# Routed attention with eight experts: three edits to the order of VectorE's weight sums and of one count

## The chip, the core and the metric

The kernel runs on one core of a Trainium2 chip. A core has five engines that work at the same time, each with an instruction queue of its own that is worked off strictly in order: TensorE (PE: matrix products, with the loading of its weights, PEld, shown apart), VectorE (DVE: elementwise work, reductions, transposes of 32x32 blocks), ScalarE (ACT: activations and copies), GpSimd (POOL: here constants, gathers and scatters by index) and SyncE (SP: starts the transfers between HBM and the on-chip memory). An engine that needs a result of another one waits for it at the head of its queue, and all that is queued behind waits too. The metric is the time of one execution on the device, in microseconds (us).

## The reference, cut to what matters

```python
# attention: batch 4, 8 heads, 768 positions, head size 64, 16 clusters per head
mask = q_assign[:, :, :, None] == k_assign[:, :, None, :]   # same nearest centroid
attn = softmax(where(mask, q @ k.T / sqrt(64), -1e9))
x = (attn @ v)                      # -> 3072 rows of 512
# experts: 8 experts, 512 -> 1024 -> 512, each row goes to one expert
logits = x @ w_gate;  e = argmax(logits);  gate = softmax(logits)[e]
out = gate * (relu(x @ w1[e]) @ w2[e])
```

All inputs and outputs are float32. How many rows each expert gets is known only while the kernel runs.

## The kernel before, in words

**Attention.** 16 head pairs are worked through one after the other; TensorE makes scores (L433), ScalarE the exponentials (L445), VectorE their sums (L451), TensorE the weighted values (L457). While the pairs run, a row's expert is chosen for each batch of 768 rows (`gate`, `choose`), and `count` (L588) and `number` (L595) give each row its place in a list per expert: `count` is two small products on TensorE over the tile `last` that `choose` leaves (L592, L593), `number` is a few small VectorE instructions on the two products and six scatters on GpSimd. For the last batch these steps lie in the expert part, in turn 0.

**Experts in turns.** Ten turns follow, `s` from 0 to 9. A turn takes one expert and a fixed number of its rows: 288 and 288 for the two early turns (chosen by the counts of the first three batches), then 256, 288, 288, 384, 416, 416, 448 and 128 for the experts in order of their counts. Turn s has

- `first_weights` and `second_weights`: SyncE fetches w1 and w2 (2 MB each) into one of two buffers, by s odd or even (L97, L105);
- `places`, `indices`, `gather`, `weigh`, `take`: the list of rows is loaded (L712, L716), VectorE turns it into indices `gi` and `si` (L728, L729), GpSimd gathers the rows (L738), VectorE scales them (`xw`, L755), SyncE stores them to HBM (`turn_rows` in HBM, L761) and loads them again in a blocked layout (`xs`, L771);
- `turn_rows`: one VectorE transpose of `xs` to `xT` (L780);
- `layer1`, then `layer2`.

**Fewer products by sums.** Both layers multiply 2x2 blocks in the seven-product form that needs sums of blocks first. All sums are VectorE instructions at L789: four of the rows (`x_sums`: `xc`), four of the first weights (`w1_sums`: a0 to a3, 128x1024 each), four of the hidden values (`h_sums`: `hs`) and four of the second weights (`w2_sums`: v0 to v3, 128x1024 each). In this order a2 comes before a1 before a3, and v0 before v1 before v3. The first layer uses d = A2 X2 first, then A1, A0 and A3; the second V2, V1, V0 and V3. Each of these tiles has one buffer, so a sum of turn s+1 also waits until turn s has used its own. Turn 0 uses the plain form in its second layer, turn 9 in both.

**Where the products meet VectorE.** In `layer1` each half j makes seven products (L969). The fifth, `product(c, A[0], X[0])`, is followed by a VectorE addition into the hidden tile `h` (L927 by way of `add`), and the seventh goes on adding into the same PSUM bank c, so it waits for that addition. `layer2` has the same shape (L1070): after the fifth product, `product(c, t[0], V[0])`, VectorE adds into `z` (L1138), and the seventh, `product(c, t[3], b22)`, waits for this addition. Those two places are where a late VectorE holds TensorE.

**What sets the order.** Apart from register loads, the order on each queue is the order in which the program calls. `layer1` and `layer2` take lists of hooks. `layer1` calls hook 0 to 6 after the seven products of the first half and 7 to 13 after those of the second, `layer2` calls 0 to 6 after the seven products of its first pair of 128-row blocks (hooks behind that follow whole 128-row blocks); in turn 0, whose second layer is plain, hooks 0 to 3 lie in the first 128-row block and 4 to 7 in the second, one after every second step. `at(h1, i, f, ...)` hangs step f of any turn on hook i of this turn's first layer, `at(h2, i, ...)` on one of its second. Steps on one hook are called in the order of their `at`. For the weight sums the hooks come from a tuple, in the order that the loop at L1220 has: a2, a1, a0, a3, v2, v0.

```python
                if GR[s + 1]["T"] >= 2 * P:
                    for (h, i), f, a in zip(when, (w1_sums,) * 4 + (w2_sums,) * 2, (2, 1, 0, 3, 2, 0)):
                        at(h, i, f, s + 1, (a,), nc.vector)
                at(h2, 1 if s == 1 else 3, turn_rows, s + 1)
                if GR[s + 1]["T"] >= 2 * P:
                    at(h2, 1 if s == 1 else 4, x_sums, s + 1)
```

So before the change VectorE works off, within `layer2` of a turn s >= 2 and for the next turn: a0 (hook 1), a3 and v2 (hook 2), the transpose `xT` (3), the addition into `z` behind the fifth product, `x_sums` and `weigh` (4), the second addition into `z`, v0 (5). In turn 0: a2 (hook 1), a1 (2), `xT` (3), `x_sums` (4), a0 (5), a3 (6), then `indices` of turn 2, v2 and v0 (7).

Of the kernel before, what the change touches and what calls it, by code (L numbers as in the profile page):

```python
# [33 lines left out]
def kernel(  # L34
# [12 lines left out]
    B, H, S, D = q.shape  # L47
# [120 lines left out]
    with tc.manual_schedule(), ExitStack() as actx:  # L168
# [596 lines left out]
        def take(s):  # L765

            g = GR[s]
            T, C = g["T"], g["C"]
            g["xs"] = xp.tile([P, T_MAX // Q4, P], F32, name="xs")
            for r in range(HP):  # L770
                nc.sync.dma_start(  # L771
                    out=g["xs"][Q4 * r : Q4 * (r + 1), 0:C, :],
                    in_=g_d[s][0:T, P * r : P * (r + 1)].rearrange("(c t) d -> t c d", t=Q4),
                )
# [120 lines left out]
    with tc.manual_schedule(), ExitStack() as ectx:  # L895
# [125 lines left out]
        def pairs_of(s):  # L1021


            return GR[s]["T"] // (2 * P) if s else 0

        def h_sums(s):

            g = GR[s]
            g["H"] = []
            for p in range(pairs_of(s)):  # L1030
                c0 = 2 * P * p
                h = g["h"]
                a11, a21 = h[:, 0:4, c0 : c0 + P], h[:, 0:4, c0 + P : c0 + 2 * P]
                a12, a22 = h[:, 4:8, c0 : c0 + P], h[:, 4:8, c0 + P : c0 + 2 * P]
                t = [hpool.tile([P, 4, P], F32, name=f"hs{i}") for i in range(4)]
                V = nc.vector
                strassen(V, t[2], a11, a21, ALU.subtract)
                strassen(V, t[0], a21, a22, ALU.add)
                strassen(V, t[1], t[0], a11, ALU.subtract)
                strassen(V, t[3], a12, t[1], ALU.subtract)  # L1040
                g["H"].append((a11, a12, a22, t))
# [119 lines left out]
        def first_weights(s):  # L1161
            if s >= len(EARLY):
                expert(s)
            GR[s]["w1"] = fetch1(GR[s]["e"], (wa, wb)[s % 2])

        def second_weights(s):
            GR[s]["w2"] = fetch2(GR[s]["e"], (wa, wb)[s % 2])

        for s in range(NS):
            h1, h2 = {}, {}  # L1170

            def at(d, i, f, *a):
                d.setdefault(i, []).append(lambda: f(*a))

            if s == 0:
                at(h1, 3, sum_up, n - 1)
                at(h1, 3, weights_of, n - 1)
                at(h1, 4, gate, B - 1)
                at(h1, 4, gate_exp, B - 1)
                at(h1, 5, gate_sum, B - 1)  # L1180
                at(h1, 5, choose, B - 1)
                at(h1, 8, count, B - 1)
                at(h1, 9, number, B - 1)
                at(h1, 11, rows, n - 1)
                at(h1, 11, store, n - 1)
                at(h1, 12, rank_all)
                at(h2, 0, rank_rest)
                at(h2, 3, places, 2)
                at(h2, 3, first_weights, 2)
                at(h2, 5, places, 3)  # L1190
                at(h2, 7, indices, 2)
                at(h2, 7, gather, 2)
            if s == 3:
                at(h1, 12, ask)
                at(h2, 4, answer)
            if s < last:
                if s == 0:
                    first_weights(1)
                elif s > 1:
                    take(s + 1)  # L1200
                if s == 1:
                    at(h1, 6, weigh, 2)
                    at(h1, 7, take, 2)
                    at(h1, 8, second_weights, 2)
                else:
                    second_weights(s + 1)
                if 0 < s <= last - 2:
                    at(h2, 0, first_weights, s + 2)

                if 0 < s <= last - 3:  # L1210
                    at(h2, 1, places, s + 3)

                if s == 0:
                    when = ((h2, 1), (h2, 2), (h2, 5), (h2, 6), (h2, 7), (h2, 7))
                elif s == 1:
                    when = ((h1, 9), (h1, 12), (h2, 2), (h2, 3), (h2, 6), (h2, 6))
                else:
                    when = ((h1, 9), (h1, 10), (h2, 1), (h2, 2), (h2, 2), (h2, 5))
                if GR[s + 1]["T"] >= 2 * P:
                    for (h, i), f, a in zip(when, (w1_sums,) * 4 + (w2_sums,) * 2, (2, 1, 0, 3, 2, 0)):  # L1220
                        at(h, i, f, s + 1, (a,), nc.vector)
# [3 lines that stand above are left out]
            if s == 0:  # L1225
                at(h1, 2, gather, 1)
                at(h1, 8, weigh, 1, slice(0, 1))
                at(h1, 11, weigh, 1, slice(1, 2))
                at(h1, 12, weigh, 1, slice(2, 3))
                at(h1, 12, take, 1)  # L1230
            elif s + 2 <= last:
                at(h1, 5 if s == 2 else 4, indices, s + 2)
                at(h1, 5 if s == 2 else 4, gather, s + 2)
                at(h2, 6 if s == 1 else 4, weigh, s + 2)
            if pairs_of(s):
                at(h1, 4, w2_sums, s, (1,), nc.vector)

                at(h1, 5 if s == 1 else 6, w2_sums, s, (3,), nc.vector)
            if s == last - 1:

                at(h1, 4, nc.gpsimd.drain)
            (layer1 if GR[s]["T"] >= 2 * P else few_columns)(s, h1)
            h_sums(s)
            layer2(s, h2)
# [271 lines left out]
```

## Time and profile before

| | |
|---|---|
| three executions | 657.41 to 657.73 us, median 657.68 us |
| the profiled execution | 657.44 us, of which the span from first to last instruction is 655.7 us |
| granted TensorE clock | 0.999 of full speed |
| attention, to the first expert product | 0 to 328.2 us of the span |
| expert part | 328.2 to 655.7 us |
| busy in the expert part (328.0 to 655.7) | PE 318.5, PEld 263.5, DVE 203.3, ACT 95.8, POOL 86.9 us |
| span behind TensorE's last product | from about 649.1 us |

How to read it: an engine's busy time is the sum of its instructions' durations, which overlap a little at their ends. TensorE's products are pipelined, their ends are modelled and reach into the next product, so what TensorE loses is read best from the distance between the starts of two groups of products: eight products with the same shape have the same distance from the start of one group to that of the next when nothing is waited for. A line of the timeline has the start, the duration (of all that is merged into the line), engine, source line, operation, the tile written and the tiles read, the shapes, the count, and in square brackets the idle time ahead of it with what ended it. a0 to a3 show as `a`, v0 to v3 as `v`, since buffer numbers are left out.

### The profile page before, as it was taken

What the parts mean: (1) busy time and instruction counts of PE and PEld (TensorE: products, weight loads), DVE (VectorE), ACT (ScalarE), POOL (GpSimd) and SP (SyncE); (2) the same over time, 40 slices, a digit from 0 to 9 for tenths busy, and PEclk for the clock granted to TensorE, in tenths of its full rate; (3) what the DMA queues carried; (4) which work ended last, traced back from release to release, by engine and by line L of the source; (5) the groups of instructions that cost most, each with busy time, mean ns of one, the idle gap of its engine ahead of it and who ended that gap; (6) DMA issues with size and microseconds to landing.
All of it is one profiled execution on the core that took longest, in us unless ns stands there. A gap on an engine that the chain in (4) does not pass through costs nothing.

```text
span 655.7 us, 11490 instructions
## 1 busy us (share of the span) xinstructions
PE 643.5 (98%) x4252; PEld 423.0 (65%) x4252; DVE 489.5 (75%) x845; ACT 338.3 (52%) x584; POOL 133.0 (20%) x166
## 2 busy tenths in 40 slices
PE   8999999999999999999999999999999999999995
PEld 4454544445444454444494989989897977869773
DVE  6988878998889988999977987888869365572300
ACT  5677877768778677867532433334241331413210
POOL 5500000022000300033013612324241422140010
PEclk9999999999999999999999999999999999999999
DMA  7753445443455433329476498667694836614010
GB/s 150 162 104 73 79 92 98 74 80 62 79 98 98 74 74 72 74 33 334 110 274 195 152 335 283 232 254 234 241 309 157 281 131 184 229 66 168 8 49 19
DMA packets 189760, 95.38 MB, mean 145 GB/s; under 512 B 152895, under 2 KB 171839, under 8 KB 188416
## 3 DMA queue, kind: packets, MB, share of 16 engines
q1 hardware_dynamic: 184624, 81.56, 45.4%
q0 software_dynamic: 4928, 12.97, 6.0%
q8 instruction: 35, 0.57, 0.4%
q14 instruction: 29, 0.24, 0.1%
q10 hardware_dynamic: 144, 0.03, 0.0%
HBM read 74.10 MB, written 20.70 MB: 145 GB/s over the span
## 4 chain that ended last, share of the span: by engine, by line
PE 94%; DVE 4%; issue 0%; ACT 0%; POOL 0%; POOLq 0%; DVEq 0%; ACTq 0%
PE sps L433 24%; PE mps L457 19%; PE bank L969 12%; PE bank L1089 10%; PE sbank L969 9%; PE bank L1070 7%; PE sbank L1070 6%; PE mps L480 3%; PE mps L291 2%; PE bank L938 1%; DVE xT L780 1%; DVE a L789 1%; DVE v L789 1%; PE sps L356 0%; PE sps L226 0%
## 5 line engine op out<-in xcount | busy, mean ns | idle before, releaser
L445 ACT ACTIVATE A<-sps 128x768 f32<-128x768 f32 x192 | 151.7, 814 | 29.1 <-PE sps L433 28.5
L433 PE MATMUL sps<-qT,kT 64*128 64x384 f32 x768 | 158.9, 492 | 0.0
L451 DVE TENSOR_TENSOR acc<-acc,A 128x768 f32<-128x768 f32 x128 | 121.3, 948 | 10.6 <-ACT A L445 2.4
L457 PE MATMUL mps<-A,v_in 128*64 128x384 f32 x768 | 127.4, 488 | 0.0
L433 PEld LDWEIGHTS sps<-qT,kT 64*128 64x128 f32 x768 | 66.8, 187 | 52.2 <-issue 46.0
L457 PEld LDWEIGHTS mps<-A,v_in 128*64 128x64 f32 x768 | 53.8, 137 | 70.6 <-issue 64.2
L1044 POOL DMA_INDIRECT out_dram<-z,si x30 | 47.1, 1571 | 195.3 <-DVE z L927 165.7
L607 POOL DMA_INDIRECT tokens_of<-tg,pos_i x24 | 28.2, 1176 | 268.5 <-DVE pos_i L605 262.4
L433 PE MATMUL sps<-mq,mk 64*128 64x384 bf16 x384 | 64.6, 323 | 1.6 <-DVE mk L383 1.0
L1089 PE MATMUL bank<-w,h 128*128 128x512 f32 (+2 forms) x224 | 64.4, 596 | 0.0
L340 ACT ACTIVATE mk<-ohT,kscn,ksc 32x384 bf16<-32x384 bf16 x60 | 42.0, 700 | 40.2 <-DVE ohT L327 36.3
L738 POOL DMA_INDIRECT xg<-x_rows,gi x30 | 40.3, 1343 | 45.8 <-DVE si L729 16.5
L969 PE MATMUL sbank<-xc,a 128*128 128x144 f32 (+4 forms) x288 | 47.9, 309 | 0.2 <-ACT sbank L1002 0.2
L969 PE MATMUL bank<-xT,w 128*128 128x144 f32 (+4 forms) x288 | 47.6, 308 | 0.0
L1089 PEld LDWEIGHTS bank<-w,h 128*128 128x128 f32 (+2 forms) x224 | 24.6, 151 | 32.5 <-issue 32.3
L969 PEld LDWEIGHTS bank<-xT,w 128*128 128x128 f32 x288 | 43.8, 190 | 2.3 <-issue 1.9
L451 DVE TENSOR_TENSOR acc<-A 128x768 f32<-128x768 f32 x32 | 30.6, 957 | 18.3 <-ACT A L445 18.2
L969 PEld LDWEIGHTS sbank<-xc,a 128*128 128x128 f32 x288 | 43.3, 190 | 0.7 <-ACT sbank L1002 0.4
L927 DVE TENSOR_TENSOR h<-sbank,p 128x288 f32<-128x288 f32 (+4 forms) x18 | 9.2, 513 | 45.3 <-PE sbank L969 43.9
L987 ACT ACTIVATE h<-h 128x288 f32<-128x288 f32 (+4 forms) x36 | 17.6, 488 | 40.2 <-DVE h L927 38.1
L433 PEld LDWEIGHTS <-mk 64*128 64x128 bf16 x384 | 19.9, 94 | 27.5 <-DVE mk L383 2.6
L755 DVE TENSOR_TENSOR xw<-xg,sf 128x256 f32<-128x256 f32 (+2 forms) x60 | 32.6, 603 | 0.2
(216 smaller groups left out, 898.7 us busy)
## 6 DMA issues: line engine op xcount, KB each, us to landing
w<-in_moe_w_dram SPq DMA_DIRECT2D x20, 2048.0 KB
v_in<-in_v_dram SPq DMA_DIRECT2D x32, 192.0 KB
x_rows<-x SPq DMA_DIRECT2D x64, 96.0 KB
turn_rows<-xw SPq DMA_DIRECT2D x23, 256.0 KB
q_in<-in_q_dram SPq DMA_DIRECT2D x60, 96.0 KB
k_in<-in_k_dram SPq DMA_DIRECT2D x60, 96.0 KB
xs<-turn_rows SPq DMA_DIRECT2D x16, 144.0 KB
xs<-turn_rows SPq DMA_DIRECT2D x8, 208.0 KB
```

The source lines that it names most:

```text
L340: nc.scalar.activation(dst, src, AF.Identity, bias=less, scale=big)
L433: nc.tensor.matmul(SP[n, h, j][:, a, 0:HS], lhsT=kt[rows, j * P : (j + 1) * P], rhs=qt[rows, h * HS : (h + 1) * HS], start=first, stop=not ...
L445: nc.scalar.activation(A[n, h, j], ps[:, :, 0:HS], AF.Exp, scale=D**-0.5)
L451: nc.vector.tensor_tensor(ACC[n, h], first, A[n, h, j], op=ALU.add)
L457: nc.tensor.matmul(O[n, h][D * a : D * (a + 1), 0:HS], lhsT=VIN[n][:, a, j, :], rhs=A[n, h, j][:, a, :], start=(j == 0), stop=(j == NQ - 1),)
L607: ins = nc.gpsimd.indirect_dma_start(out=t_d[:, :], out_offset=bass.IndirectOffsetOnAxis(ap=pos_i[:, i : i + 1], axis=0), in_=tg[:, b, i, ...
L738: nc.gpsimd.indirect_dma_start(out=xg[0:m], out_offset=None, in_=x_d[0:rows_in, :], in_offset=bass.IndirectOffsetOnAxis(ap=g["gi"][0:m, j ...
L755: nc.vector.tensor_tensor(xw[0:m, :, :, d2 * a : d2 * (a + 1)], xg[0:m].rearrange("p (r a d b) -> p a r b d", r=HP, a=2, b=DB)[:, a], g["s ...
L969: nc.tensor.matmul(ps[:, f * T2 : (f + 1) * T2], lhsT=w[:, k, (2 * j + f) * P : (2 * j + f + 1) * P], rhs=x[:, k, :], start=first and f + ...
L1044: ins = nc.gpsimd.indirect_dma_start(out=out[:, :], out_offset=bass.IndirectOffsetOnAxis(ap=GR[s]["si"][0:rows, j : j + 1], axis=0), in_=z ...
L1070: nc.tensor.matmul(ps[:, 0:H], lhsT=x[:, k, :], rhs=y[:, k, :], start=first and k == 0, stop=k == 3, skip_group_check=not first,)
L1089: nc.tensor.matmul(ps[i * m : (i + 1) * m, :], lhsT=h[:, f, j * P : j * P + m], rhs=w[:, f, :], start=(k == 0), stop=(k == FB // n - 1),)
```

## The change

Three edits, all in the loop over the turns; no instruction is added or taken away, and no shape is changed.

1. Turn 0, first layer: `count` of the last batch goes from hook 8 to hook 9 and `number` from 9 to 10. On TensorE the two small products now follow the third product of the second half instead of preceding it; the order on the other engines does not change by this.
2. Turn 0, second layer, sums for turn 1: a1 goes from hook 2 to 1, a0 from 5 to 2, a3 from 6 to 2, v2 from 7 to 6. VectorE now has a2, a1, a0, a3, then `xT`, the additions into `z`, `x_sums`, v2, the indices of turn 2, v0.
3. Turns s >= 2, second layer, sums for turn s+1: v2 goes from hook 2 to 5, v0 from 5 to 6. VectorE now has a0, a3, `xT`, the addition into `z`, `x_sums`, `weigh`, the second addition into `z`, v2, v0.

The sums in turn 1 (for turn 2) stay where they are. SyncE's order differs at one place: in turn 3 the three stores of weighed rows now stand ahead of a register load for the branch at the end (L1249). GpSimd's and ScalarE's order does not change.

```diff
-                at(h1, 8, count, B - 1)
-                at(h1, 9, number, B - 1)
+                at(h1, 9, count, B - 1)
+                at(h1, 10, number, B - 1)
...
                 if s == 0:
-                    when = ((h2, 1), (h2, 2), (h2, 5), (h2, 6), (h2, 7), (h2, 7))
+                    when = ((h2, 1), (h2, 1), (h2, 2), (h2, 2), (h2, 6), (h2, 7))
                 elif s == 1:
                     when = ((h1, 9), (h1, 12), (h2, 2), (h2, 3), (h2, 6), (h2, 6))
                 else:
-                    when = ((h1, 9), (h1, 10), (h2, 1), (h2, 2), (h2, 2), (h2, 5))
+                    when = ((h1, 9), (h1, 10), (h2, 1), (h2, 2), (h2, 5), (h2, 6))
```

## The prediction

> **What bounds the kernel now.** First the page: busy time by engine and the chain that ended last.
>
> ```profile
> PE 643.5 (98%) x4252; PEld 423.0 (65%) x4252; DVE 489.5 (75%) x845; ACT 338.3 (52%) x584; POOL 133.0 (20%) x166
> ...
> PE 94%; DVE 4%; issue 0%; ACT 0%; POOL 0%; POOLq 0%; DVEq 0%; ACTq 0%
> ```
>
> TensorE is busy for 98% and is 94% of the chain; the 4% of VectorE in it are places where TensorE waited for VectorE. So an edit that only moves VectorE work is worth what it adds to or takes from TensorE's waits. The waits of TensorE between 328 and 656 us are few:
>
> ```profile
> PE sbank L1070 <- DVE z L927: 1.2, 4, 0.4
> PE mps L592 <- DVE last L586: 0.6, 1, 0.6
> PE sbank L969 <- DVE h L927: 0.5, 1, 0.5
> ```
>
> A fourth row is 0.2 us behind ScalarE. These three are the places that the three edits touch. Then I read the timeline at each. Turn 0, TensorE alone:
>
> ```profile
> 336.61 1.14 PE L969 MATMUL bank<-xT,w 128*128 128x144 f32 x8
> 337.59 1.14 PE L969 MATMUL bank<-xc,a 128*128 128x144 f32 x8
> 339.33 0.17 PE L592 MATMUL mps<-last,lt_b 128*128 128x8 bf16 x1 [0.59 <-DVE last L586]
> 339.35 0.17 PE L593 MATMUL mps<-last,ones_b 128*128 128x8 bf16 x1
> 339.38 1.23 PE L969 MATMUL sbank<-xc,a 128*128 128x144 f32 x8
> ```
>
> Groups of this shape start 0.98 us apart (336.61, 337.59); the one around the count starts 1.79 later. Now VectorE from turn 0 into turn 1:
>
> ```profile
> 355.81 1.38 DVE L780 STREAM_TRANSPOSE xT<-xs 128x1152 f32<-128x1152 f32 x1 [3.67 <-DMA xs<-turn_rows]
> ...
> 361.52 1.22 DVE L789 TENSOR_TENSOR a<-w 128x1024 f32<-128x1024 f32 x1
> 362.65 1.22 DVE L789 TENSOR_TENSOR a<-w,a 128x1024 f32<-128x1024 f32 x1
> ...
> 363.93 2.35 DVE L789 TENSOR_TENSOR v<-w 128x1024 f32<-128x1024 f32 x2
> 366.20 0.45 DVE L927 TENSOR_TENSOR h<-sbank,p 128x288 f32<-128x288 f32 x1
> ```
>
> And TensorE over the same stretch:
>
> ```profile
> 365.05 1.14 PE L969 MATMUL bank<-xc,w 128*128 128x144 f32 x8
> 366.71 1.25 PE L969 MATMUL sbank<-xT,a 128*128 128x144 f32 x8 [0.52 <-DVE h L927]
> ```
>
> VectorE idles 3.67 us for the rows, later does four sums in a row, and the addition into h behind them holds TensorE: 1.66 from start to start instead of 0.98. Last, a later turn (4), VectorE and then TensorE:
>
> ```profile
> 466.27 1.21 DVE L789 TENSOR_TENSOR v<-w 128x1024 f32<-128x1024 f32 x1
> 467.40 1.76 DVE L780 STREAM_TRANSPOSE xT<-xs 128x1536 f32<-128x1536 f32 x1
> 469.10 0.37 DVE L927 TENSOR_TENSOR z<-sbank,p 128x256 f32<-128x256 f32 x1
> ```
>
> ```profile
> 467.19 1.89 PE L1070 MATMUL bank<-v,h 128*128 128x256 f32 x8
> 469.52 1.99 PE L1070 MATMUL sbank<-w,hs 128*128 128x256 f32 x8 [0.44 <-DVE z L927]
> ```
>
> 2.33 from start to start, where 1.73 is usual for this shape. The idle column says 0.44, since the modelled end reaches 0.16 into the next group; starts are the better measure, and I use them.
>
> **Edit 1, the count.** 1.79 - 0.98 = 0.81 us lost, of which about 0.1 are the two products themselves, which stay. `last` is ready at 339.27; one group later TensorE arrives at 338.57 + 0.98 = 339.55. So 0.70 goes. What comes behind: `number` starts on VectorE with `base` at 340.22, behind a row weighing that ends at 340.32; the counts will be done near 339.85, so that weighing hides them with 0.4 to spare. Without it VectorE would wait, and with it the transpose and store of the attention rows, by at most the 0.98 of the group. Gain 0.70.
>
> **Edit 2, turn 1's sums.** a0 and a3 leave the place behind `x_sums` (two starts 1.13 apart, 2.27 in all) and fall into the 3.67 idle: a2 starts at 349.68, a1 1.24 later at 350.92, and with two more starts 1.13 apart and 1.22 for the last the four end at 354.4, 1.4 before the rows arrive. Were the rows there already, `xT` would come up to 2.27 later than it could. a0 and a3 wait only for turn 0's first layer, over at 344.4. v2 passes ahead of the indices of turn 2, but these still come 2.27 - 1.13 = 1.14 earlier. The addition into h is wanted at the end of the fifth group, 364.07 + 1.14 = 365.2; VectorE gets there at 366.20 - 2.27 = 363.9. So the whole 1.66 - 0.98 = 0.68 goes, and 1.3 of margin stays for TensorE being 0.70 earlier. A rule of the Trainium skill speaks against this: VectorE: DVE Perf Modes, section "The DRAIN you can't avoid", gives each VectorE instruction a flush of its duration less 266 ns before the next one. Taken as added to the row's 1.21, four sums would take 4 x (1.21 + 0.94) = 8.6 us and end at 358.3, 2.5 behind the rows, and turn 1's second product, which needs `x_sums`, would be late by about as much, 2 us at most. The rows decide: 361.52 and 362.65 start 1.13 apart, so nothing is added.
>
> **Edit 3, v2 behind the rows' turning.** Excess of the seventh group of layer 2, start to start less 1.73: turn 2 0.30 (410.38, 412.40), turn 3 0.08, turn 4 0.61, turn 5 none, turn 6 0.38 (538.89, 541.00), turn 7 0.51 (580.08, 582.32). Together 1.88. v2 takes 1.13 ahead of `xT`, in turn 2 also 1.95 of waiting for w2. Without it `xT` ends at about 468.0 in turn 4, the addition into z at 468.3, and TensorE wants it at 468.92; turns 2, 3, 6 and 7 come out with 0.7 to 1.1 to spare. The rows must be there: in turns 2 to 4 their load is issued 13.9 to 20 us before `xT`, and in turn 0 it took 4.5. What is next late: v2 and v0 now stand back to back ahead of the next turn's addition into h, but `weigh` too is about 1.13 earlier. In turn 3, with the distances of today's rows: a3 ends at 437.9, `xT` at 439.2, the addition into z waits for its product until 439.37, the small steps of `answer` and `x_sums` put `weigh` at 442.0, the second addition at 445.2, v2 at 445.5, v0 at 446.65, and it ends at 447.87; the addition into h is wanted at 447.96 - 0.08 = 447.88. The same sum gives v0's end at 418.5 in turn 2 (wanted 419.1) and 476.8 in turn 4 (wanted 477.5); turns 5 to 7 have a whole 128-row block (6.9 us) in between. Turn 3 is a tie, and its addition has about 0.2 to give before TensorE feels it (done at 448.42, next group at 448.67). Cost 0; with no cover at all it is 1.13 for each of the three turns.
>
> **Queues.** The moved sums issue no DMA. On SyncE three stores pass a register load that waits until 441.2; the stores go at 444.11: nothing. On GpSimd the scatter behind the addition into z now meets v2 and v0. The Trainium skill's page SBUF — State Buffer, section "Who interferes with whom", infers that tensor_tensor leaves GpSimd's writing of descriptors alone; here scatters beside sums back to back take 3.92 us (435.91) where 0.97 is usual. By the rule the next gathers come when they do now, by the row up to 3 us later; rows gathered are weighed some 10 to 20 us later, so both give 0. Only turn 2's gather is close: 5.7 us from indices to weighing, of which both ends move up by 1.1 to 1.4.
>
> **Sum.** 0.70 + 0.68 + 1.88 = 3.26. Profiled execution 657.44 - 3.26 = 654.18; it lies 0.24 under the median of the runs, so the median should be 657.68 - 3.26 = 654.4. Turn 1's own wait (385.34 to 387.39, 0.32) and one for ScalarE in turn 3 (0.37) stay; if they go too, 653.7.
>
> **Rivals.** *A, all seven waits go*: 654.4. *B, the lead of 1.38 from turns 0 and 1 is given back in turn 2*: its v2 waits for w2 until 388.18, so VectorE is tied to a transfer there. If w2 doesn't come earlier, `weigh` and the addition into h follow it and TensorE waits. For it: DMA share 0.90 from 374.5 to 389. Against: w2's issue (377.69) stands behind the row stores and loads of `weigh`, which moves up 1.3. Time 654.4 + 1.4 = 655.8. *C, the change does less than it says*: the waits are worth only the idle column, 0.59 + 0.52 + 0.44 + 0.22 + 0.35 = 2.12, and B happens to the first two (1.11): 657.68 - 1.01 = 656.7. Against: distances between starts are longer. *D, slower*: transfers, not VectorE, set when `xT` starts. Then it stays where it is, the old waits stay, and v0 ends 1.13 later, less VectorE's present idle before h, 0.74, 0.32 and 0.76: 0.39 + 0.81 + 0.37 = 1.57, so 659.2. It decides from the point where the rows land within 0.3 us of today's `xT`; the 13.9 us and more speak against it, what speaks for it is DMA share 0.96 in turn 2.
>
> **Numbers.** A 0.62, B 0.17, C 0.11, D 0.10. Below 657.68 by over 0.2% (1.3 us, about what can be told from no change) are A and B, 0.79; C within, 0.11; D 0.10. The range goes from 653.6 (A with the two waits that stay) to 656.8 (through B and C).
>
> **What would show it.** Right: the three VectorE rows of TensorE's waits gone or down to turn 1's; the count with no idle before it; 0.98 into the seventh group of turn 1; `xT` of turn 4 right behind a3; VectorE with idle ahead of the next h. Wrong: `xT` waiting for the rows in turns 2 to 7, TensorE waiting for h in turns 2 to 5, or v of turn 2 waiting longer for w2.

## The result, and the profile after

The median goes from 657.69 us (six executions, 657.08 to 658.26) to 653.73 us (six, 652.92 to 654.72): ratio 0.994, 95% interval 0.9928 to 0.9952, or 3.96 us less. The profiled execution took 653.81 us, with a span of 652.0.

The page's rows on busy time and on the chain that ended last, after:

```profile
PE 642.6 (99%) x4252; PEld 423.6 (65%) x4252; DVE 490.1 (75%) x845; ACT 339.1 (52%) x584; POOL 138.9 (21%) x166
...
PE 97%; DVE 1%; issue 0%; POOL 0%; POOLq 0%; ACT 0%; DVEq 0%
```

No engine does less work. VectorE's share of the chain fell from 4% to 1% and TensorE's rose from 94% to 97%: what went is waiting. TensorE's waits between 326 and 656 us, after:

```profile
PE sbank L1070 <- DVE z L927: 0.2, 1, 0.2
```

One row is left of the three (and the one behind ScalarE): turn 1's own wait, which the edits do not touch. The count in turn 0, TensorE:

```profile
339.33 1.14 PE L969 MATMUL sbank<-xc,a 128*128 128x144 f32 x8
340.31 0.17 PE L592 MATMUL mps<-last,lt_b 128*128 128x8 bf16 x1
340.34 0.17 PE L593 MATMUL mps<-last,ones_b 128*128 128x8 bf16 x1
340.37 1.23 PE L969 MATMUL bank<-xT,w 128*128 128x144 f32 x8
```

The two small products have no idle ahead of them. From 339.33 to 340.37 are 1.04 us where 1.79 were. VectorE from turn 0 into turn 1:

```profile
353.23 1.22 DVE L789 TENSOR_TENSOR a<-w,a 128x1024 f32<-128x1024 f32 x1
355.85 1.38 DVE L780 STREAM_TRANSPOSE xT<-xs 128x1152 f32<-128x1152 f32 x1 [1.39 <-DMA xs<-turn_rows]
...
365.32 0.46 DVE L927 TENSOR_TENSOR h<-sbank,p 128x288 f32<-128x288 f32 x1 [1.27 <-PE sbank L969]
```

The sums a0 (at 352.10) and a3 (the first line) now lie in what was VectorE's idle time ahead of the rows. The addition into h has 1.27 us of idle ahead of it, put down to TensorE: now VectorE waits for TensorE. Over the same stretch TensorE starts its groups 0.98 apart, the one that waited among them:

```profile
365.05 1.14 PE L969 MATMUL bank<-xc,w 128*128 128x144 f32 x8
366.03 1.14 PE L969 MATMUL sbank<-xT,a 128*128 128x144 f32 x8
```

Last, turn 4, VectorE and then TensorE:

```profile
463.12 1.21 DVE L789 TENSOR_TENSOR a<-w,a 128x1024 f32<-128x1024 f32 x1
464.26 1.76 DVE L780 STREAM_TRANSPOSE xT<-xs 128x1536 f32<-128x1536 f32 x1
465.95 0.37 DVE L927 TENSOR_TENSOR z<-sbank,p 128x256 f32<-128x256 f32 x1
...
475.76 0.56 DVE L927 TENSOR_TENSOR h<-sbank,p 128x384 f32<-128x384 f32 x1 [0.42 <-PE sbank L969]
```

```profile
465.54 1.89 PE L1070 MATMUL bank<-v,h 128*128 128x256 f32 x8
467.26 1.89 PE L1070 MATMUL sbank<-w,hs 128*128 128x256 f32 x8
```

`xT` follows a3 without v2 in between, the seventh group starts 1.72 behind the sixth instead of 2.33, and the two v sums, now back to back from 473.00, end early enough that the next addition into h still waits 0.42 for its product.

**Where the 3.96 came from.** I laid the two traces side by side by the starts of TensorE's groups. From the first expert product to turn 9's first product (L938), which is what "the expert part" means from here on, before took 306.54 us and after 302.30, 4.24 less. The attention ahead of it was 0.76 longer in this profile, which is no work of the change (last section), and what lies behind it was 0.21 shorter; so the spans differ by 3.69. The table is of these two executions, not of the medians.

| place | forecast | measured |
|---|---|---|
| count, turn 0 | 0.70 | 0.75 |
| turn 1, addition into h | 0.68 | 0.78 |
| turn 2, addition into z | 0.30 | 0.40 |
| turn 3, addition into z | 0.08 | 0 |
| turn 4 | 0.61 | 0.72 |
| turn 6 | 0.38 | 0.49 |
| turn 7 | 0.51 | 0.62 |
| seven places | 3.26 | 3.76 |
| turn 3, TensorE behind ScalarE's copy (L1002) | 0 | 0.48 |

Turn 3's 0.08 was no wait: the same 1.81 from start to start stands in after and in every other trace.

### The profile page after: what moved, and what is told of

It reads as the page before. It is cut to its first block, busy times and chain, and to the rows that moved or that the text cites. A ratio compares the mean times of both kernels' runs of the same rounds, so it can differ in the third digit from the quotient of the medians.

```text
span 652.0 us, 11484 instructions
## 1 busy us (share of the span) xinstructions
PE 642.6 (99%) x4252; PEld 423.6 (65%) x4252; DVE 490.1 (75%) x845; ACT 339.1 (52%) x584; POOL 138.9 (21%) x166
## 4 chain that ended last, share of the span: by engine, by line
PE 97%; DVE 1%; issue 0%; POOL 0%; POOLq 0%; ACT 0%; DVEq 0%
PE sps L433 25%; PE mps L457 19%; PE bank L969 13%; PE bank L1089 10%; PE sbank L969 10%; PE bank L1070 8%; PE sbank L1070 6%; PE mps L480 3%; PE mps L291 2%; PE bank L938 1%; PE sps L226 0%; PE sps L356 0%; DVE a L789 0%; DVE mk L383 0%; DVE ge L311 0%
## 5 line engine op out<-in xcount | busy, mean ns | idle before, releaser
L1044 POOL DMA_INDIRECT out_dram<-z,si x30 | 51.9, 1731 | 188.4 <-DVE z L927 161.5
L607 POOL DMA_INDIRECT tokens_of<-tg,pos_i x24 | 29.8, 1241 | 270.1 <-DVE pos_i L605 264.0
```

The lines of the kernel that those rows point to most:

```text
L607: ins = nc.gpsimd.indirect_dma_start(out=t_d[:, :], out_offset=bass.IndirectOffsetOnAxis(ap=pos_i[:, i : i + 1], axis=0), in_=tg[:, b, i, ...
L1044: ins = nc.gpsimd.indirect_dma_start(out=out[:, :], out_offset=bass.IndirectOffsetOnAxis(ap=GR[s]["si"][0:rows, j : j + 1], axis=0), in_=z ...
```

## The experiments

The theory at this point: the three edits act at separate places, and each place is a wait of TensorE that vanishes once VectorE arrives in time. The rivals: the lead is given back at a later place, and VectorE's new order has no slack at the next h. All kernels compute the whole reference. Medians are given beside that of the kernel before on the same chip, and the length of the expert part (before 306.54, after 302.30) from each one's profile.

**Each edit alone, and all.** The edits are those of the change, one at a time.

```diff
 e1: edit 1 alone          e2: edit 2 alone (s == 0)        e3: edit 3 alone (s >= 2)
+at(h1, 9, count, B - 1)   +when = ((h2,1),(h2,1),          +when = ((h1,9),(h1,10),
+at(h1, 10, number, B - 1)          (h2,2),(h2,2),                   (h2,1),(h2,2),
                                    (h2,6),(h2,7))                   (h2,5),(h2,6))
```

> Edit 1 alone. My theory: TensorE's waits add up one by one, so this is the 0.70 us of the forecast, or 0.75 with the 0.1 by which the two profiles show a group behind a wait to start later than usual: 0.7 to 0.8 us under the kernel before. Rival (the lead is given back): TensorE meets VectorE's addition into h in turn 1 earlier, VectorE is no earlier there, so the wait of 0.68 grows by what is gained here and the gain is near 0. In the trace turn 1's seventh group would start 1.66 behind the sixth by the first and some 2.3 by the second.

> Edit 2 alone. My theory: 0.68 to 0.78 us under the kernel before, seventh group of turn 1 at 0.98 behind the sixth, count as before with 0.59 of idle. Rival: turn 2 is tied to the landing of its second weights (v of turn 2 waited until then) and gives it back: near 0, and TensorE waits in turn 2's first layer. The wait of 0.37 for ScalarE in turn 3 is touched by no edit: if it is chance, it is missing here or stands elsewhere; if it belongs to the old order of v0 and v2, it is here again.

> Edit 3 alone. My theory: the waits before the seventh group of the second layer go in turns 2, 4, 6 and 7, by starts 1.88 with turn 3's 0.08, by the two profiles 2.2: 1.9 to 2.3 us under the kernel before; if the wait for ScalarE in turn 3 hangs on v2's place, 2.6. Rival (transfers set when the rows are turned): xT starts no earlier, the gain is 0 or a loss. Second rival: only turn 2, where v2 waited 1.95 for w2, is worth something: 0.4.

> The change as a whole again, beside its parts on one chip. If the waits are independent, its distance to the kernel before is the sum of the three parts within their spread: 3.3 to 4.2 us under it. If a lead is given back somewhere, it is clearly less than the sum; if one edit opens room for another, clearly more.

| kernel | median (range, executions) | ratio to before (657.68) | expert part |
|---|---|---|---|
| edit 1 | 656.62 (655.49 to 657.73, 21) | 0.998 (0.9971 to 0.9989) | 305.76 |
| edit 2 | 656.23 (655.12 to 657.71, 14) | 0.9982 (0.9971 to 0.9992) | 304.61 |
| edit 3 | 655.22 (654.12 to 656.03, 8) | 0.9965 (0.9952 to 0.9977) | 303.46 |
| all | 654.11 (653.36 to 654.26, 5) | 0.9944 (0.9929 to 0.996) | 302.60 |

The medians of the parts add up to 1.06 + 1.45 + 2.46 = 4.97; the whole is 3.57, within the 3.3 to 4.2 expected if the waits are independent. The kernel before spreads over 3.6 us in its 37 executions, so this alone says little; the traces show more, but each is one execution. Edit 1 alone takes its 0.76 at the count and gives most of it back in turn 1. TensorE's wait for h with edit 1 alone:

```profile
PE sbank L969 <- DVE h L927: 0.8, 1, 0.8
```

The wait for h was 0.5 before. TensorE is ahead, and VectorE is not, since it hangs on the rows. VectorE with edit 1 alone:

```profile
355.54 1.38 DVE L780 STREAM_TRANSPOSE xT<-xs 128x1152 f32<-128x1152 f32 x1 [3.92 <-DMA xs<-turn_rows]
```

It waits 3.92 us for the rows instead of 3.67. By the clock of the span `xT` starts 0.27 earlier than before, and TensorE's group ahead of the wait 0.57 earlier (364.48 instead of 365.05); the difference, 0.30, is what the wait has grown by. In turn 1's second half TensorE loses 0.27 more (372.43 to 373.58 where 0.98 is usual, 0.10 behind it): there the addition into h stands behind a weighing that waited 0.35 for gathered rows. So 0.57 of the 0.76 go in turn 1 of this trace. Its expert part is 0.78 shorter all the same, but 0.48 of that is turn 3's wait for ScalarE, which is absent, and 0.14 a shorter stall in turn 2.

Edit 2 takes the 0.78 in turn 1. The rest of its 1.93 in the trace lies in turns 2, 3 and 4 (0.31, 0.48, 0.36), which it does not touch. Edit 3 gives 2.2 at its four places (0.40, 0.72, 0.48, 0.61). Its trace is 3.08 shorter: turn 3's wait for ScalarE is absent (0.48), and turn 1's wait too (0.69), with the rows transposed at 354.99, 0.8 earlier than before, and no edit made there; 0.33 came in turn 1's second half, as with edit 1.

With all three edits again (e4) the expert part is 0.30 longer than in the first profile of the change, by a new wait behind turn 4. TensorE with e4:

```profile
476.79 1.57 PE L969 MATMUL sbank<-xT,a 128*128 128x192 f32 x8
```

The group ahead starts at 475.29: 1.50 where 1.30 is usual, and 0.11 more behind it. VectorE's addition into h (476.20) has no idle ahead of it here, where it had 0.42 above, since in `weigh` VectorE waited 1.16 (to 472.54) for a store of weighed rows, with v2 and v0 queued behind. So the cover of edit 3 does not always hold.

**One sum more.** Does each place hang on VectorE's order alone, to the tenth of a us? With all three edits in, a3 is computed a second time ahead of `xT` (e5), or v0 a second time ahead of the next h (e6), for s >= 2. Both are extra work.

```diff
 e5:
+                    if s >= 2:
+                        at(h2, 2, w1_sums, s + 1, (3,), nc.vector)
 e6:
+                    if s >= 2:
+                        at(h2, 6, w2_sums, s + 1, (0,), nc.vector)
```

> The changed kernel, but in turns 2 to 7 a3 is computed twice, right ahead of xT: 1.13 us of VectorE time in the place that v2 left, and v2 and v0 still behind the weighing. My theory (what costs is VectorE time ahead of the addition into z): the waits of turns 2 to 7 come back except for turn 2's wait on w2, that is 0.6 in turn 4, 0.5 in 6 and 0.6 in 7, none in turn 2, 1.7; and v0 ends 1.13 later ahead of h, which TensorE feels in turns 3 and 4 by 0.3 to 1.0 each: 2.2 to 3.5 us over the changed kernel, so between the kernel before and 1.5 us under it. Rival (it was v2's wait for its transfer, or v2's place for other reasons): no more than 0.5 over the changed kernel.

> The changed kernel, but in turns 2 to 7 v0 is computed twice, ahead of the next turn's addition into h: tests the cover that edit 3 rests on. In the changed kernel's trace VectorE idles 0.49 ahead of h behind turn 2, 0.0 behind turn 3 and 0.42 behind turn 4, and h is done about 0.2 before TensorE needs it. My theory: 1.13 more costs 1.13 - 0.49 - 0.2 + 0.1 = 0.5, 1.0 and 0.6, and nothing behind turns 5 to 7 where a whole 128-row block lies between: 2.1 us over the changed kernel. Rival (the cover is wider than reckoned, or the delay is taken up later): under 0.5; second rival (each of six turns pays): 6 x 1.13 = 6.8.

The kernel before has 657.83 on this chip, for e7 and e8 too. e5: median 656.37 (0.9976, 0.9966 to 0.9985), expert part 304.88, or 2.58 over after. e6: 656.14 (0.998, 0.9973 to 0.9987), expert part 305.00, or 2.70 over after, where 2.1 was expected. TensorE's waits with the second a3:

```profile
PE sbank L1070 <- DVE z L927: 1.2, 4, 0.5
```

The old row is back, with v2 still out of the way: turn 1's wait and those of turns 4, 6 and 7 (0.21, 0.34 and 0.48 idle). One sum of 1.13 us ahead of `xT` is enough for that, whichever it is; a new wait for h behind turn 3 (0.65 + 0.11 from starts) comes on top. With the second v0 the wait for h is:

```profile
PE sbank L969 <- DVE h L927: 1.9, 3, 0.8
```

Three waits, behind turns 2, 3 and 4, and none behind turns 5 to 7, as the block of rows that lies between had said. VectorE at the middle one:

```profile
444.51 3.63 DVE L789 TENSOR_TENSOR v<-w 128x1024 f32<-128x1024 f32 x3
448.06 0.45 DVE L927 TENSOR_TENSOR h<-sbank,p 128x288 f32<-128x288 f32 x1
```

Three sums and then h with no idle ahead of it. From starts the three cost 0.51, 0.94 and 0.95, and 0.11 more behind each. So the slack that the change leaves ahead of h in these turns is below one sum.

**Turn 1's remaining wait, and half of edit 2.** e7 takes a3, computed in turn 1 for turn 2, from ahead of the additions into z to behind both (`xT` and `x_sums` come before either place); e8 moves only a0 into turn 0's idle time and leaves a3 and v2 where they were.

```diff
 e7 (s == 1):
-                    when = ((h1, 9), (h1, 12), (h2, 2), (h2, 3), (h2, 6), (h2, 6))
+                    when = ((h1, 9), (h1, 12), (h2, 2), (h2, 5), (h2, 6), (h2, 6))
 e8 (s == 0):
-                    when = ((h2, 1), (h2, 1), (h2, 2), (h2, 2), (h2, 6), (h2, 7))
+                    when = ((h2, 1), (h2, 1), (h2, 2), (h2, 6), (h2, 7), (h2, 7))
```

> The changed kernel, and in turn 1 too a sum goes behind the addition into z: a3 for turn 2 from hook 3 to hook 5. TensorE's last wait for VectorE in the expert part (seventh group of turn 1's second layer, 2.05 where 1.73 is usual) should go: 0.3 to 0.4 us under the changed kernel, 4.3 under the kernel before. Rival: a3 then stands with v2 and v0 ahead of the weighing and of h of turn 2, where VectorE has 0.3 of idle; if that is what is next late, the wait moves there and nothing is won.

> The changed kernel with half of edit 2: only a0 goes ahead of the rows of turn 1, a3 stays behind them. VectorE idles 1.27 ahead of turn 1's h in the changed kernel, so a delay of 1.13 just fits. My theory (a wait is a threshold, not a price per instruction): within 0.1 us of the changed kernel. Rival (each sum in front of h costs its share): 0.4 over it.

e7: median 653.97 (0.9948, 0.9935 to 0.9961), expert part 302.51: no gain. Turn 1's wait is gone (0.43) and another stands behind it, TensorE with e7:

```profile
392.48 1.06 PE L969 MATMUL bank<-xc,w 128*128 128x128 f32 x8
393.90 1.16 PE L969 MATMUL sbank<-xT,a 128*128 128x128 f32 x8 [0.37 <-DVE h L927]
394.90 1.06 PE L969 MATMUL bank<-xT,w 128*128 128x128 f32 x8
```

1.42 and 1.00 from start to start where 0.89 is usual: 0.53 + 0.11 lost. The wait has moved from the addition into z to the next turn's addition into h. e8: median 653.51 (0.994, 0.9927 to 0.9952), expert part 302.31 against 302.30. VectorE with e8:

```profile
364.76 0.46 DVE L927 TENSOR_TENSOR h<-sbank,p 128x288 f32<-128x288 f32 x1 [0.34 <-PE sbank L969]
```

One sum in the idle time is enough: h is in time with 0.34 to spare instead of 1.27. The gain of edit 2 is a threshold, not a slope.

**Following the wait one step further, and the change without edit 3.** e9 is e7 with v0 of turn 2 moved from turn 1's second layer into turn 2's first layer. e10 has edits 1 and 2 only. e11 is the kernel before once more, for one look at how much its own trace varies.

```diff
 e9 (on e7): (h2, 6) for v0 of turn 2 dropped in the s == 1 tuple, and
+            if s == 2:
+                at(h1, 4, w2_sums, s, (0,), nc.vector)
             if pairs_of(s):
                 at(h1, 4, w2_sums, s, (1,), nc.vector)
```

> The changed kernel with a3 of turn 1 behind the additions into z (as in the run that moved it alone, where the wait of 0.43 went from z in turn 1 to h in turn 2, +0.64) and v0 for turn 2 moved on, behind turn 2's first addition into h and right ahead of v1, which is the first to need it. My theory (the wait moved because v2, v0 and the weighing together stand ahead of h): both waits go, expert part 0.4 us shorter than the changed kernel's, 0.06%, which the trace can show and the times hardly. Rival: v0 and v1 back to back delay the second addition into h and the hidden sums, and a wait comes up there: no gain.

> Edits 1 and 2 without 3. The count alone gained 0.76 at its place, and TensorE gave most of it back in turn 1, where the rows landed no earlier by as much. Theory (edit 2 is the cover that lets the count's gain stand): the count's 0.76 and turn 1's 0.78 both stand in the trace with no give-back in turn 1, expert part 303.9 us from its first product to turn 9's first, 0.7 shorter than with edit 2 alone. Rival (the rows' landing bounds turn 1 whatever VectorE does): 304.6, as with edit 2 alone.

> The kernel before, unchanged, one more profile. The profile that the forecast was made from has a wait of TensorE for ScalarE in turn 3 (L1002, 0.48 with the late start behind it) that no run since has shown, and a wait of 0.68 in turn 1 that was 0 in one run with the same order up to there. If the first is chance it is missing here: expert part 306.06 instead of 306.54 us. If turn 1's wait follows the landing of the rows, it changes with the start of xT, by as much.

e9: median 654.13 (0.9933, 0.9916 to 0.995; before on this chip 658.73), expert part 302.86: no gain again. Both old waits are gone and a third came. From the timeline of all engines with e9, ScalarE and TensorE:

```profile
395.70 0.42 ACT L987 ACTIVATE h<-h 128x256 f32<-128x256 f32 x1 [2.05 <-DVE h L927]
...
396.72 1.16 PE L969 MATMUL sbank<-xc,a 128*128 128x128 f32 x8 [0.73 <-ACT sbank L993]
```

The second addition into h starts at 395.25, behind v0 and v1; ScalarE's activation at the head of its queue waits 2.05 for it, the copy L993 (396.29) stands behind that, and TensorE waits for the copy. In this stretch each move of a VectorE sum changed who waits, and none made the wait go.

e10: median 656.76 (0.9969, 0.996 to 0.9977), expert part 306.19, where both expectations lay between 303.9 and 304.6: a miss for both. Count (0.76) and turn 1 (0.77) both stand, so edit 2 is the cover that edit 1 alone lacked. But the lead does not last. VectorE and then TensorE in turn 2 with e10:

```profile
409.21 1.22 DVE L789 TENSOR_TENSOR v<-w 128x1024 f32<-128x1024 f32 x1 [2.84 <-DMA w<-in_moe_w_dram]
```

```profile
409.18 1.89 PE L1070 MATMUL bank<-v,h 128*128 128x256 f32 x8
412.09 1.99 PE L1070 MATMUL sbank<-w,hs 128*128 128x256 f32 x8 [1.02 <-DVE z L927]
413.92 1.14 PE L969 MATMUL bank<-xT,w 128*128 128x144 f32 x8
```

v2 for turn 3 needs w2, which was issued at 397.99 and lands near 409.2. VectorE waits 2.84 us for it with `xT` (410.35) and the addition into z (411.65) queued behind, and TensorE, early, waits 1.02: from 409.18 to 412.09 are 2.91 instead of 1.73. Before, the same place lost 0.30. The lead of TensorE did not make this transfer land earlier by as much: issue 397.99 instead of 398.80, v2 at 409.21 instead of 409.52. A wait of 0.77 behind ScalarE (L1002) in turn 3 takes the rest. e10's profiled execution (657.34) is one of its longer ones, so the sizes are those of one execution. The median lies 1.97 under that of before on this chip (1.5 to 2.6 by the interval), which is no less than the 1.38 forecast for edits 1 and 2: that the lead is lost on average is not shown. In the changed kernel w2 is issued at 398.00 and v2 stands behind `weigh`, at 415.39: no wait.

e11 took 658.27 us, with an expert part of 306.97, where 306.06 was expected: a miss. Turn 1's wait does follow the rows, VectorE with e11:

```profile
356.24 1.38 DVE L780 STREAM_TRANSPOSE xT<-xs 128x1152 f32<-128x1152 f32 x1 [3.51 <-DMA xs<-turn_rows]
```

Counted from the first expert product (329.00), `xT` starts 0.17 earlier than in before, and the wait for h is 0.52 by starts instead of 0.68. Turn 2's loss has another place: 0.31 and 0.14 ahead of two additions into h, none ahead of z. Turn 3's wait for L1002 is gone from the idle column only: its group still starts 0.24 late (425.19 to 426.41), when that copy ends, and ahead of it is another stall of 0.33 (422.80 to 424.11 where 0.98 is usual) that the profile puts down to "issue". So turn 3 stalls in before, e10 and e11 in three sizes, with edits 1 or 2 alone it does not, and in none of the eight traces with edit 3. In the three, ScalarE's copy L998 and VectorE's next sum a2 start at one moment, both put down to a product of TensorE, 0.19, 0.87 and 1.21 us after the modelled end of that product; with edit 1 alone it is 0.04. The granted clock is 1.00 in all four. So the lateness does not seem to begin in ScalarE's queue.

## Why the forecast held, step by step

**Held.** *The mechanism*: six of the seven VectorE waits were there, and all six are gone from both traces of the change; e5 brings three of them back with one sum. *Edit 1*: 0.70 forecast, 0.75 came, and `number` cost nothing, as forecast. *Edit 2*: a0 and a3 fit into the idle time; 1.3 us of margin less 0.70 for an earlier TensorE was the forecast, 1.27 came, since the rows too came earlier by nearly the count's 0.75. *The rule on the flush behind a VectorE instruction* (the Trainium skill, VectorE: DVE Perf Modes, "The DRAIN you can't avoid") added nothing here: the four sums end at 354.45, against 354.4 forecast from the row and 358.3 from the rule read as an addition. *Edit 3's cover*: 0.6, 0 and 0.7 of slack ahead of h behind turns 2, 3 and 4 were forecast; VectorE's idle there is 0.49, 0 and 0.42 in the trace, and e6, which takes 1.13 from it, brings three waits. Turn 3 was called a tie; its h starts with no idle ahead of it, and TensorE does not wait. Turn 4's 0.7 was not enough in e4. *Queues*: scatters beside back-to-back sums are slow, as the row said. GpSimd in turn 2, after:

```profile
415.74 2.89 POOL L1044 DMA_INDIRECT out_dram<-z,si  x1 [15.76 <-DVE z L927]
```

2.89 us beside v2 and v0, of which 1.99 pass until v0 ends and 0.90 behind it; 1.75 before, 0.85 and 0.90; 0.97 where no sum runs. So it looks as if the scatter stood still until the sums were through. The section that the forecast drew on (the Trainium skill, SBUF — State Buffer, "Who interferes with whom") also states that a VectorE instruction with two inputs in SBUF contends with a GpSimd instruction that reads SBUF; the sums have two such inputs, the scatter is given its indices `si` as a tile, and these times agree with it better than with the inference about descriptors. Which part of the scatter is held is not shown. It did not reach the path: TensorE's waits above show nothing of it.

**Off in size.** The terms were taken as the late start of one group, and the group behind it was left out. It too starts 0.10 to 0.11 late: in e7 1.00 instead of 0.89, in e10 1.83 (412.09 to 413.92) instead of 1.73. With that, five terms come out larger: turns 1 and 2 by 0.10, 4, 6 and 7 by 0.11. The count is 0.05 larger, and turn 3's 0.08 was a misreading: 1.81 from start to start is what that place takes without a wait. 0.50 in all, 3.76 instead of 3.26.

**Right by chance.** 0.48 more went with the ScalarE wait of turn 3, which the forecast let stay. No edit moves an instruction there. A stall of this kind is in three of the five traces without edit 3 (before, e10, e11) and in none of the eight with it, so neither chance nor a link to v2's place is excluded; what causes it stays open. The 653.7 named for the case that both remaining waits go meets the measured 653.73 by luck: turn 1's stayed, and the rest came from the sizes above.

**Wrong.** The sum took the edits as independent. The medians do not speak against that, but in the traces they are not: edit 1 alone gives back most of its gain in turn 1 (e1), edits 1 and 2 give theirs back in turns 2 and 3 (e10), and with v2's new place the lead lasts (after, e4). Rival B (the lead is given back to w2 in turn 2) named the right kind of place, but I weighed it against turn 3's weights too little: I looked at the w2 that turn 2 itself uses, which came 2.27 earlier (issue 375.42 instead of 377.69) since its queue moved up. The one that bites is the next turn's, fetched during turn 2, and edit 3 takes exactly that wait off the path. Rival C (only the idle column counts) is refuted by the sums of starts: each wait is worth more than its idle, not less. Rival D needs `xT` to wait for rows in turns 2 to 7; turn 4's row above shows `xT` right behind a3, and in turns 2, 3, 5, 6 and 7 it starts likewise right behind a3 (406.71, 436.18, 492.85, 535.24, 575.94).

**A better version?** e8 (ratio 0.994), the change (0.994), e7 (0.9948) and e9 (0.9933) cannot be told apart by their intervals. None of the runs beats the change beyond them.

## What to carry to other kernels

A wait at the head of an in-order queue is a threshold: once the late engine arrives in time, further moves bring nothing (e8), and the next instruction in line sets how far the gain goes (e7, e9). Value an edit not only at its own place: follow the lead that it makes to the next place tied to a transfer, and ask whether that place moves up too; if it does not, the lead can be lost there, as in the traces of e1 and e10, unless the instruction that waits is taken off the path. Measure a stall from starts and include the group behind it.

## What the runs showed of the hardware that was not expected

- A group of products behind a wait of TensorE is followed 0.10 to 0.11 us late: 1.08 for 0.98 and 1.00 for 0.89 in layer 1, 1.83 for 1.73 in layer 2. Instruction by instruction, it is the first of the eight products that is longer: 0.23 to the next instead of 0.12 (before, 425.38; e10, 425.73).
- The start of the attention differs between executions of any order. The stretch from 14 to 20 us, after (columns: window and length, busy time of PE, PEld, DVE, ACT and POOL with counts, granted clock, DMA share, GB/s):

```profile
14.00:20.00 6.00, 5.52 (x30) 3.07 (x30) 5.58 (x9) 3.32 (x5) 5.37 (x13) 0.72 0.32 85
```

  TensorE's granted clock was 0.72 there in after's profile and 1.00 in before's, with 30 TensorE instructions where before has 37. It is no matter of the change: e11, the kernel before, has 0.72 too, and e4, the changed kernel, 1.00. The first expert product starts at 329.16 in after, 328.40 in before, 329.00 in e11 and 328.97 in e4, so the clock in this stretch does not account for all of it. That is why the expert part, not the span, is compared above.
- The order without the change varies more: on one chip 34 executions of before lie within 4.0 us (655.62 to 659.63), 22 of e6, which holds the three edits and one sum more, within 1.7 (655.18 to 656.90). That more of before's waits hang on the landing of transfers would explain it; this is argued, not shown, and e4 has such a wait with the change in.
